# Sums of keys and values stored in whole rows and rearranged later, and two tiles of the last stage weighted and scaled in the third pass

## The chip, the cores and the metric

One core of one Trainium2 chip runs the kernel. The metric is the device time of one execution, in microseconds (us). The engines are TensorE (PE in the profile), VectorE (DVE), ScalarE (ACT), GpSimd (POOL) and SyncE (SP), which issues all the DMAs; SPq is its queue.

## What is computed

```python
x  = A_x                                   # 2048 x 1024
xn = layernorm(x)
q, k, v = split_heads(xn @ wqkv)           # 32 heads of 32
pq, pk  = q @ w_phi, k @ w_phi             # per head
phi_q = concat(softmax(pq), softmax(-pq))  # 64 features a head
phi_k = concat(softmax(pk), softmax(-pk))
kv  = phi_k^T v                            # per head, summed over all rows
z   = sum over rows of phi_k
s   = ((phi_q kv) / (phi_q z + 1e-6)) @ wo
g   = silu((silu(xn @ w1) * (xn @ w3)) @ w2)
out = x + s * g
```

All in float32. A row of `x` needs `kv` and `z`, which are sums over all rows; so the queries' side can only be finished when all keys have been seen.

## The kernel before

The 2048 rows are 16 tiles of 128. The tiles go in eight pairs, `pairs = (0,4), (1,5), (2,6), (3,7), (8,12), (9,13), (10,14), (11,15)`: all large products are done by a recursion that makes the four blocks of a 2 x 2 product from seven products (A11, A12, S2, S1, S3, S4, A22, in this order in the gate and the passes). Each operand is split in a high and a low part, and three products of the parts are added up.

The stages, in order of time:

- **Gate and up** (to about 1180 us): the hidden layer, written to memory as `h_d`. Beside it weights are folded, split and stored.
- **Three passes** (`c` = 0, 1, 2; about 1180 to 1690 us). Passes 0 and 1 make keys and values of half of the heads each, and add up `kv` and `z` in one PSUM bank, `pkv`, by small matmuls (`kv`, L625). Pass 2 makes the queries. For each pair seven operands of 512 KB (`xoA`, `xoS`) are reloaded by `reload` (L521), always one pair ahead. They live in a pool of 11 buffers (`quad`). A pair is seven products of 12 matmuls; bank b is added to by A11, S2, S3 and A22, bank c by S1 and S4, and in between ACT or DVE must have read the partial result.
- `kv_out` (L725) writes out `pkv` when the next pass has got to the product S1 of its first pair: ACT copies the sums of key times value to `kva`, DVE those of the keys to `zs`, and the SP queue stores them in sixteen pieces, eight to `kv_d` and eight to `z_d` (L735, L736), in the order in which the last stage reads them. The stores to `z_d` are element by element, as rows become columns.
- In pass 2, `spikes` (L681) takes a half of a tile's projected queries, subtracts the largest and the smallest of each head (L685 to L689), takes exponents on ACT (L690) and stores the result `e` to `e_d` (L691).
- **Down** (about 1690 to 2234 us): 56 steps (`r`), seven slices of the hidden layer by eight pairs. A step is again seven products, of six matmuls, into banks that DVE, ACT and POOL add to `acc` (L935 to L941). `a_first` and `a_second` load (`hr`, L767) and split (L90, L91) the next step's operands. The other operands (`bo`) come by `load_b` (L760) into a ring of buffers. In the last slice (`end`, steps 48 to 55) each finished pair is gated (`gate`, L870) and stored, and between the steps the first two tiles of the last stage are prepared: `load_e`, `weigh` (POOL, L886, `e` times `z`), `add_up` (DVE, L894), `factors` (L901 to L906) and `scale` (L912, one half on DVE, one on POOL).
- **Last stage** (from about 2234 us): for each tile, `e` scaled is transposed (`turned`, L1036), multiplied with `kvu`, the rearranged sums (L1049), then with `wo` (L1063), and gated and added to `x` (`result`). Tile i+2 is added up and scaled and tile i+3 weighted while tile i is multiplied.

What sets the order: in gate and up, in the last step of down, and in the last stage the order on the engines is the order of the code (`in_order`). In the passes and in most of down the builder orders each engine's instructions ahead of time by its own estimates of when they are ready, earlier code first. The SP queue issues its DMAs strictly one after the other: one that has to wait, for a buffer, for data or for an earlier DMA to land, holds all behind it.

## Time and profile before

| | |
|---|---|
| median of 3 runs | 2474.27 us (2473.87 to 2474.87) |
| the profiled execution | 2471.39 us |
| its span, first to last instruction | 2469.6 us |
| mean granted TensorE clock | 0.994 |
| busy: PE, DVE, ACT, POOL | 2385.4, 1686.7, 901.4, 726.3 us |
| DMA moved | 584.99 MB, mean 237 GB/s |

The profile is of one execution. A row of a timeline gives start and length in us, the engine, the line of the kernel, the operation, output and input by the program's names, shapes and count, and in brackets the time that the engine was idle before and what it waited for. A row of grouped instructions gives, behind the bar, busy us in all and mean ns of one, and behind the second bar the idle time before them. A row of stretches gives start and end, length, the busy time of PE, weight loads, DVE, ACT and POOL with the number of instructions, the granted clock, the share of time in which the DMA engines were busy, and GB/s. The chain of waits gives start, length and what it was that the end hung on. Banks are named banka, bankb, bankc.

### The profile page before, as it was taken

The numbers are of one execution on the slowest core, as the hardware profiler recorded it, in microseconds if no ns is written. First come the engines' busy times: TensorE is split into PE (matmuls) and PEld (weight loads), VectorE is DVE, ScalarE is ACT, GpSimd is POOL, SyncE is SP. The second block draws the span as 40 slices with busy tenths as digits, with TensorE's granted clock in tenths as the row PEclk, the third lists the DMA queues.
The fourth block names the chain that finished last, engine by engine and source line by source line (L and its number), as shares of the span: only waits on it lengthen the run. The fifth ranks groups of instructions, "written<-read, shape, count | busy, mean of one in ns | idle before, by whom it ended". The sixth has DMA issues, their size and how long they took to land.

```text
span 2469.6 us, 35815 instructions
## 1 busy us (share of the span) xinstructions
PE 2385.4 (97%) x13552; PEld 1954.8 (79%) x13552; DVE 1686.7 (68%) x2471; ACT 901.4 (36%) x1564; POOL 726.3 (29%) x521
## 2 busy tenths in 40 slices
PE   6999999999999999999999999999999999989999
PEld 5888877788777887878788788787888888867887
DVE  8656777774476777774576565566678787896764
ACT  6544544443344444543221111234322222333221
POOL 2233455553355555541000000000011111154663
PEclk9999999999999999999999999999999999999999
DMA  7566688866886776775998778897442344556553
GB/s 263 176 223 222 222 279 292 293 227 210 258 282 238 264 260 244 271 242 194 363 353 338 257 246 303 312 352 266 176 169 94 140 178 171 184 187 237 192 186 111
DMA packets 291196, 584.99 MB, mean 237 GB/s; under 512 B 25808, under 2 KB 140496, under 8 KB 288336
## 3 DMA queue, kind: packets, MB, share of 16 engines
q1 hardware_dynamic: 291024, 582.71, 67.6%
q8 instruction: 107, 1.75, 0.3%
q14 instruction: 65, 0.53, 0.1%
HBM read 377.88 MB, written 204.74 MB: 236 GB/s over the span
## 4 chain that ended last, share of the span: by engine, by line
PE 69%; DMA 11%; DVE 7%; issue 6%; POOL 4%; SPq 1%; ACT 1%; DVEq 0%; ACTq 0%; POOLq 0%
PE bankb L556 18%; PE bankb L929 11%; PE bankb L639 9%; PE bankc L556 8%; PE bankc L929 6%; PE banka L556 4%; PE bankc L639 4%; PE banka L929 3%; PE banka L639 2%; POOL ez L886 2%; PE pm L1063 2%; DVE bo L91 2%; DMA xoA<-xo_d0A 1%; POOL e L912 1%; DMA wkv_d0T<-wkvo 1%
## 5 line engine op out<-in xcount | busy, mean ns | idle before, releaser
L91 DVE TENSOR_TENSOR bo<-rw,bo 128x512 fp32r<-128x512 f32 x336 | 295.2, 880 | 146.1 <-ACT bo L90 143.9
L939 POOL TENSOR_TENSOR acc<-acc,u 128x512 f32<-128x512 f32 x48 | 63.8, 1330 | 604.2 <-ACT u L938 604.2
L90 ACT CAST bo<-rw 128x512 fp32r<-128x512 f32 x336 | 205.8, 621 | 48.6 <-PE bankc L556 5.0
L929 PE MATMUL bankb<-bo,as 128*128 128x512 f32 x816 | 201.4, 389 | 2.1 <-DVE acc L941 2.1
L268 POOL TENSOR_TENSOR rw<-rw,t 128x512 f32<-128x512 f32 x56 | 79.3, 1416 | 379.0 <-DVE bo L91 378.9
L1063 PE MATMUL pm<-wos,oT 128*128 128x512 f32 x768 | 182.9, 394 | 0.0
L929 PEld LDWEIGHTS bankb<-bo,as 128*128 128x128 f32 x816 | 153.4, 188 | 34.5 <-DVE acc L941 2.5
L556 PE MATMUL bankb<-op1A,bo 128*128 128x512 f32 x672 | 161.3, 396 | 11.7 <-DVE u L584 8.5
L556 PE MATMUL bankb<-op0A,bo 128*128 128x512 f32 x672 | 160.0, 392 | 8.8 <-DVE u L584 8.4
L1063 PEld LDWEIGHTS pm<-wos,oT 128*128 128x128 f32 x768 | 141.9, 188 | 31.6 <-issue 3.0
L556 PE MATMUL bankb<-op0S,bo 128*128 128x512 f32 x672 | 163.4, 392 | 1.9 <-ACT u L575 1.8
L556 PE MATMUL bankc<-op0S,bo 128*128 128x512 f32 x672 | 163.3, 391 | 2.0 <-ACT u L582 1.4
L556 PE MATMUL bankc<-op1S,bo 128*128 128x512 f32 x672 | 161.8, 390 | 3.1 <-ACT u L582 1.9
L556 PE MATMUL bankb<-op1S,bo 128*128 128x512 f32 x672 | 161.5, 389 | 0.4 <-ACT u L575 0.4
L556 PEld LDWEIGHTS bankb<-op1A,bo 128*128 128x128 f32 x672 | 127.2, 191 | 42.9 <-DVE u L584 12.9
L556 PEld LDWEIGHTS bankb<-op0A,bo 128*128 128x128 f32 x672 | 125.1, 188 | 37.8 <-DVE u L584 11.7
L556 PEld LDWEIGHTS bankc<-op1S,bo 128*128 128x128 f32 x672 | 125.9, 188 | 30.4 <-ACT u L582 2.8
L556 PEld LDWEIGHTS bankb<-op0S,bo 128*128 128x128 f32 x672 | 125.0, 188 | 29.1 <-ACT u L575 3.4
L556 PEld LDWEIGHTS bankc<-op0S,bo 128*128 128x128 f32 x672 | 125.3, 188 | 28.6 <-ACT u L582 1.8
L929 PE MATMUL bankc<-bo,as 128*128 128x512 f32 x576 | 146.6, 389 | 1.4 <-DMA bo<-w_d0B 1.4
L556 PEld LDWEIGHTS bankb<-op1S,bo 128*128 128x128 f32 x672 | 126.1, 188 | 26.9 <-ACT u L575 0.8
L929 PEld LDWEIGHTS bankc<-bo,as 128*128 128x128 f32 x576 | 108.0, 188 | 24.5 <-DMA bo<-w_d0B 1.8
(230 smaller groups left out, 4695.8 us busy)
## 6 DMA issues: line engine op xcount, KB each, us to landing
rw<-in_w SPq DMA_DIRECT2D x112, 512.0 KB, 5.0
h_d<-h SPq DMA_DIRECT2D x112, 256.0 KB, 7.1
hr<-h_d SPq DMA_DIRECT2D x56, 512.0 KB, 3.7
xoS<-xo_d0S SPq DMA_DIRECT2D x48, 512.0 KB, 9.0
xoS<-xo_d1S SPq DMA_DIRECT2D x48, 512.0 KB, 7.4
xoA<-xo_d0A SPq DMA_DIRECT2D x36, 512.0 KB, 9.1
xoA<-xo_d1A SPq DMA_DIRECT2D x36, 512.0 KB, 5.8
e_d<-eq SPq DMA_DIRECT2D x32, 512.0 KB, 5.5
```

The source lines that it names most:

```text
L90: nc.scalar.copy(hi, src)
L91: (by or nc.vector).tensor_sub(lo, src, hi.bitcast(F))
L268: nc.gpsimd.tensor_sub(b11, b22, t2)
L556: nc.tensor.matmul(bank[b], bo[bn][:, w, k], ao[an][:, u, k], start=first and n == 0, stop=LAST[b] == an and n == 11, skip_group_check=True)
L639: nc.tensor.matmul(bank[b], xo[an][:, u, k], wb[bn][:, w, k], start=an in ("A11", "A12", "S1") and n == 0, stop=LAST[b] == an and n == 11, ...
L886: nc.gpsimd.tensor_mul(t, es[i][c], zb[c])
L912: eng.tensor_mul(e3, e3, f.rearrange("p h s -> p (h s)").unsqueeze(2).to_broadcast([P, H, DH]))
L929: nc.tensor.matmul(bank[b], t[:, u, pos + k], bos[kb, bn, k][:, w], start=first and n == 0, stop=LAST[b] == an and n == 5, skip_group_chec ...
L939: nc.gpsimd.tensor_add(c, c, u)
L1063: nc.tensor.matmul(p, oT[k // 4][:, a, k % 4], wos[c, k][:, b], start=n == 0, stop=n == 23)
```

## The change

First, `kv_out` stores whole rows: `kva` in one store to `kv_d[c]`, and the sums of the keys after a transpose on PE (into the free end of the same PSUM bank) and a copy on ACT, in two stores to `z_d` with 32 contiguous numbers each. Sixteen transfers from memory to memory, one in each of steps 8 to 23 of down, bring the sums of key times value from `kv_d` to the order of `kvu_d`, from which `kvu` is loaded, one step later than before (`i == 5`).

Second, the order of tiles in the last stage becomes 3, 9, 0, 1, 2, 4, ... (`TILES`), and the first two, which are the first tiles of pairs 3 and 5, are weighted, added up and scaled in pass 2: `z` is loaded at the beginning of pair 2 into two buffers of the ring, POOL multiplies, and four pieces of vector work (`sum_e`, `sum_ez`, `factors`, `scale`) are queued in `later` and taken up one at each product. Their `e` lies in two other buffers of the ring and is stored when it is scaled. The ring's loads for down that used these buffers (`load_b(0, 2)` and `load_b(0, 3)`, until now in pairs 3 and 4) go to the last pair. The work on the first two tiles leaves the last slice of down; the weighting of the third tile moves from step 55 to the start of the last stage.

```diff
-    kv_d = dram.tile([2, 2, DH, 2 * G, DH], F, name="kv_d")
+    kv_d = [dram.tile([P, 8, DH], F, name=f"kv_d{c}") for c in range(2)]
+    kvu_d = dram.tile([P, 2 * G, DH], F, name="kvu_d")
...
     def kv_out(c, pkv):
         kva = work.tile([P, 8, DH], F, name="kva", tag="w")
         zs = small.tile([P, 8], F, name="zs")
+        zr = small.tile([8, P], F, name="zr", tag="sums")
         nc.scalar.copy(kva, pkv[:, :, :DH])
...
         nc.vector.tensor_copy(zs[:, 4:], pkv[:, 4:, DH])
+        nc.tensor.transpose(zt[0], zs, ident)
+        nc.scalar.copy(zr, zt[0])
+        nc.sync.dma_start(kv_d[c], kva)
         for s in range(2):
-            for j in range(4):
-                sl = slice(32 * j, 32 * j + 32)
-                nc.sync.dma_start(kv_d[j % 2, s, :, G * c + j // 2:G * c + G:2], kva[sl, 4 * s:4 * s + 4])
-                nc.sync.dma_start(z_d[0, c, :, j, s].rearrange("g f -> f g"), zs[sl, 4 * s:4 * s + 4])
+            nc.sync.dma_start(z_d[0, c, :, :, s], zr[4 * s:4 * s + 4].rearrange("g (j f) -> g j f", f=DH))
...
+    def spikes(t, c, p, e, scaling=False):
...
         nc.scalar.activation(e, e, AF.Exp)
-        nc.sync.dma_start(e_d[t][c], e)
+        if not scaling:
+            nc.sync.dma_start(e_d[t][c], e)
+            return
+
+        ef = e.rearrange("p (h f) -> p h f", f=DH)
+        ez = flat(quad("ez", F).rearrange("p u k t -> p (u k) t"))
...
+        nc.gpsimd.tensor_mul(ez, e, early["z"][c])
...
+        def scale():
+            nc.vector.tensor_mul(ef, ef, by.rearrange("p h s -> p (h s)").unsqueeze(2).to_broadcast([P, H, DH]))
+            nc.sync.dma_start(e_d[t][c], e)
+
+        later.extend((sum_e, sum_ez, factors, scale))
+
+    EARLY = (3, 5)
...
-                        if c == 2 and 0 < i < 5:
+                        if c == 2 and i in (1, 2):
                             load_b(0, i - 1)
+                        if c == 2 and end:
+                            load_b(0, 2)
+                            load_b(0, 3)
+                    if later:
+                        later.pop(0)()
...
+    TILES = [pairs[i][0] for i in EARLY]
+    TILES += [t for t in range(NT) if t not in TILES]
...
+        if 8 <= r < 24:
+            c, j, s = (r - 8) // 8, (r - 8) // 2 % 4, r % 2
+            q = 64 * (j % 2) + 32 * s
+            nc.sync.dma_start(kvu_d[q:q + 32, G * c + j // 2:G * c + G:2], kv_d[c][32 * j:32 * j + 32, 4 * s:4 * s + 4])
...
             elif i == 2:
                 load_e(0)
-            elif i == 3:
-                weigh(0, 0, "1")
-                weigh(0, 1, "5")
-                add_up(0, 0)
             elif i == 4:
-                add_up(0, 1)
-                factors_early(0)
                 load_e(1)
                 load_e(2)
+            elif i == 5:
                 kvu = accp.tile([P, 2 * G, DH], F, name="kvu", tag="acc3")
-                nc.sync.dma_start(kvu, kv_d.rearrange("a s f g d -> (a s f) g d"))
-            elif i == 5:
-                scale(0, 0, nc.vector)
-                scale(0, 1, nc.gpsimd)
-                weigh(1, 0, "7")
-                add_up(1, 0)
-            elif i == 6:
-                weigh(1, 1)
-                add_up(1, 1)
-                factors_early(1)
-            elif i == 7:
-                scale(1, 0, nc.vector)
-                scale(1, 1, nc.gpsimd)
-                weigh(2, 0)
-                weigh(2, 1)
+                nc.sync.dma_start(kvu, kvu_d)
...
     load_e(3)
+    weigh(2, 0)
+    weigh(2, 1)
```

More of the change, by code (lines that the diff above doesn't have):

```diff
@@ L626, in kv @@
                                  v[:, 4 * (m % 4) + h], start=first and m == 0, stop=last, skip_group_check=True)
-    pkv = None
+    pkv, zt = None, []
     def seven(xo, wb):
@@ L679, in heads @@
         return pkv, False, last, e1, v1
-    def spikes(t, c, p, e):
+    early, later = {}, []
+    def spikes(t, c, p, e, scaling=False):
         mm = small.tile([P, 2, 16], F, name="mm2")
@@ L690, in spikes, with sum_e, sum_ez, factors @@
         nc.scalar.activation(e, e, AF.Exp)
-        nc.sync.dma_start(e_d[t][c], e)
+        if not scaling:
[3 more added lines that the diff above has]
+        ez = flat(quad("ez", F).rearrange("p u k t -> p (u k) t"))
+        if c == 0:
+            early["s"] = small.tile([P, 2, 2, 16, 2], F, name="sums"), small.tile([P, 2, 16, 2], F, name="by")
+        sm, by, rho = early["s"][0][:, c], early["s"][1][:, c], small.tile([P, 2, 16], F, name="rho")
+        nc.gpsimd.tensor_mul(ez, e, early["z"][c])
+        def sum_e():
+            nc.vector.tensor_reduce(sm[:, 0].rearrange("p h s -> p (h s)"), ef, axis=AX.X, op=OP.add)
+        def sum_ez():
+            nc.vector.tensor_reduce(sm[:, 1].rearrange("p h s -> p (h s)"), ez.rearrange("p (h f) -> p h f", f=DH),
+                                    axis=AX.X, op=OP.add)
+        def factors():
+            nc.vector.reciprocal(rho[:, 0], sm[:, 0, :, 1])
+            nc.vector.tensor_mul(rho[:, 0], sm[:, 0, :, 0], rho[:, 0])
+            nc.vector.tensor_mul(rho[:, 1], sm[:, 1, :, 1], rho[:, 0])
+            nc.vector.tensor_add(rho[:, 1], sm[:, 1, :, 0], rho[:, 1])
+            nc.vector.reciprocal(by[:, :, 0], rho[:, 1])
+            nc.vector.tensor_mul(by[:, :, 1], by[:, :, 0], rho[:, 0])
+        def scale():
[3 more added lines that the diff above has]
+    EARLY = (3, 5)
+    def load_z(two):
+        for c in range(2):
+            nc.sync.dma_start(two[c], z_d[:, c].rearrange("o g j s f -> o (g j s f)").to_broadcast([P, D]))
     def queries(i, xo, wb, steps, pend):
         t0, t1 = pairs[i]
+        if i == EARLY[0] - 1:
+            early["z"] = [flat(bpa.tile([P, 2, 512], R, name="ze", tag=f"ra{6 + c}").bitcast(F)) for c in range(2)]
+            load_z(early["z"])
         for an, pb in seven(xo, wb):
@@ L702, in queries @@
                 e01 = rwp.tile([P, 2, 1024], F, name="eq", tag="rw")
-                spikes(t0, 0, k0, e01[:, 0])
+                if i in EARLY:
+                    early["e"] = [flat(bpa.tile([P, 2, 512], R, name="ee", tag=f"ra{4 + a}").bitcast(F)) for a in range(2)]
+                spikes(t0, 0, k0, early["e"][0] if i in EARLY else e01[:, 0], i in EARLY)
             elif an == "S2":
@@ L841, in tile_kernel @@
             pend = (queries if c == 2 else heads)(i, xo, wb, steps(), pend)
+            assert not (end and later)
             xo = nxt
```

27 lines of the change are left out of this document (13 added, 14 removed).

## The prediction

> **What bounds the kernel now.** I read the page first, then busy time by stretches, then the timelines of the stretches in which TensorE (PE) is not always busy.
>
> ```profile
> PE 2385.4 (97%) x13552; PEld 1954.8 (79%) x13552; DVE 1686.7 (68%) x2471; ACT 901.4 (36%) x1564; POOL 726.3 (29%) x521
> ...
> 1360.00:1525.00 165.00, 158.97 (x1592) 128.74 (x1591) 92.14 (x127) 28.71 (x39) 1.95 (x15) 0.98 0.72 250
> 1525.00:1700.00 175.00, 169.37 (x855) 138.84 (x854) 109.71 (x181) 56.21 (x73) 0.00 (x0) 0.98 0.88 325
> 1700.00:2160.00 460.00, 460.00 (x2030) 380.60 (x2029) 356.07 (x611) 140.43 (x267) 54.81 (x42) 1.00 0.46 167
> 2160.00:2234.51 74.51, 65.02 (x275) 51.75 (x273) 64.81 (x87) 26.94 (x39) 32.82 (x23) 0.98 0.59 206
> ```
>
> Columns: stretch, its length, busy PE, PEld, DVE, ACT, POOL, granted clock, DMA share, GB/s. PE is busy 97% of the span, so only what makes it wait is worth anything. Between 1700 and 2160 it never waits. It is idle for 6.0 us and 5.6 us in the two stretches in which the sums are written out, at a lower granted clock, and for 9.5 us in the end of down. The change touches just these three.
>
> The first two are one story, told by the SP queue:
>
> ```profile
> 1360.00:1370.00 10.00, 9.12 (x162) 7.18 (x160) 4.40 (x8) 2.05 (x4) 0.13 (x1) 1.00 1.00 417
> 1380.00:1390.00 10.00, 10.00 (x106) 8.12 (x105) 6.50 (x9) 2.24 (x3) 0.13 (x1) 1.00 0.09 8
> 1550.00:1560.00 10.00, 10.00 (x46) 8.29 (x45) 1.99 (x4) 2.24 (x3) 0.00 (x0) 1.00 0.15 15
> ...
> 1368.87 0.32 SPq L735 DMA_DIRECT2D kv_d<-kva  x1
> 1372.49 0.30 SPq L736 DMA_DIRECT2D z_d<-zs  x1
> ...
> 1385.68 4.04 SPq L736 DMA_DIRECT2D z_d<-zs  x1
> 1389.82 0.85 SPq L521 DMA_DIRECT2D xoA<-xo_d0A  x2
> ...
> 1389.82 9.06 DMA xoA<-xo_d0A
> 1561.93 7.73 DMA xoA<-xo_d0A
> ...
> 1398.92 5.33 PE L639 MATMUL bankb<-op3B,xoA 128*128 128x512 f32 x12 [5.16 <-DMA xoA<-xo_d0A]
> 1569.80 5.22 PE L639 MATMUL bankb<-op4B,xoA 128*128 128x512 f32 x12 [4.12 <-DMA xoA<-xo_d0A]
> 1575.01 2.72 PE banka L639 x12
> ```
>
> From 1368.87 to 1389.72 the queue issues sixteen small stores, and DMA is busy 9% of 1380 to 1390 and 15% of 1550 to 1560: the queue is stuck, not the memory. The reload of the next pair's operands stands behind them, is issued at 1389.82, lands after 9.06 us, and PE waits 5.16 us. The second time it is issued at 1561.93 and PE waits 4.12 us. After each wait twelve matmuls take 5.33 and 5.22 us where the next twelve take 2.72.
>
> The third is the last round of down:
>
> ```profile
> 2172.87 1.52 PE L929 MATMUL banka<-bo,af 128*128 128x512 f32 x6
> 2182.39 1.52 PE L929 MATMUL banka<-bo,af 128*128 128x512 f32 x6
> ...
> 2218.55 1.52 PE L929 MATMUL banka<-bo,af 128*128 128x512 f32 x6
> 2223.39 2.92 PE L929 MATMUL bankc<-late,as 128*128 128x512 f32 x6 [3.31 <-DVE acc L941]
> ...
> 2233.14 1.53 PE L929 MATMUL bankb<-bo,as 128*128 128x512 f32 x6
> ...
> 2209.62 5.21 POOL L886 TENSOR_TENSOR ez<-e,zb 128x1024 f32<-128x1024 f32 x2 [2.10 <-DVE sums L894]
> 2210.06 2.50 DVE L91 TENSOR_TENSOR as<-s,as 128x512 fp32r<-128x512 f32 x1
> ...
> L894 DVE TENSOR_REDUCE sums<-e 128x32 f32<-128x1024 f32 x4 | 4.8, 1209 | 0.0
> L894 DVE TENSOR_REDUCE sums<-ez 128x32 f32<-128x1024 f32 x4 | 4.8, 1209 | 0.5 <-POOL ez L886 0.5
> L781 DVE TENSOR_TENSOR s<-hr,sm 128x256 f32<-128x256 f32 x5 | 4.6, 924 | 0.0
> L912 DVE TENSOR_TENSOR e<-e,by 128x1024 f32<-128x1024 f32 x2 | 2.4, 1208 | 0.0
> ...
> L781 DVE TENSOR_TENSOR s<-hr,sm 128x256 f32<-128x256 f32 x42 | 17.6, 419 | 0.0
> ```
>
> A step of down is 9.52 us (2172.87 to 2182.39). The next three should put banka at 2210.95; it comes at 2218.55. DVE is why: it carries 12.0 us of adding up and scaling for tiles 0 and 1 (4.8 + 4.8 + 2.4), and its SBUF-only operations stretch while POOL weighs (as<-s 2.50 us, the L781 form 924 ns on average against 419 ns earlier in down).
>
> **The change, part by part.**
>
> *Sums stored whole.* Per write-out, sixteen stores become three: one of whole rows and two of the transposed sums. The fourth store of before goes out at 1372.49, so the queue is free for the reload then, or at the latest 3 × 4.04 us after 1368.87 = 1381.0, if each new store is held as the worst old one. Plus 9.06 us, the operand lands between 1381.6 and 1390.1, and PE needs it at 1398.92 − 5.16 = 1393.76. Both ends are in time. In the third pass the reload also stands behind the pair's own e stores, so it gains less; half of the old hold is enough, as PE was only 4.12 us short. So I take both waits and both slow restarts as gone: 5.16 + (5.33 − 2.72) + 4.12 + (5.22 − 2.72) = 14.4 us. Late next are the operands of the pair's later products, each needed 2.72 us after the one before, from a memory that was idle till now.
>
> *The transpose on PE.* Twice, a product with 128 columns, and a wait for the vector copy of the sums.
>
> ```profile
> L731 DVE COPY zs<-pkv x2: 150/152/153, 1364.1 to 1538.8; 128x4 f32<-128x4 f32 x2
> 1362.21 0.70 PE pkv L625 x59
> 1537.50 0.77 PE L625 MATMUL pkv<-ev 128*32 128x34 f32 x64
> L1036 PE MATMUL pt<-ident,e 128*128 128x128 f32 x256 | 34.1, 276 | 3.0 <-ACT et L1038 2.1
> ```
>
> A transpose is 0.28 us. If PE kept program order it would also wait from the end of the small products to the end of that copy: 1364.25 − 1362.91 = 1.3 us and 1538.95 − 1538.27 = 0.7 us. No order is written by hand in the passes, and the products of S3 are ready, so I expect them to fill the wait: −0.6 us, bounds −0.6 and −2.6.
>
> *Rearranging beside down.* Sixteen memory-to-memory transfers, one in each of steps 8 to 23, in the SP queue ahead of the next step's loads. PE is never idle in that stretch (460.00 of 460.00). No row shows such a transfer. An issue costs 0.30 to 4.04 us by the old stores, in a step of 9.52 us: 0, with a bound of nothing below it, and if the cover went, at most 4.04 us a step.
>
> *Tiles 3 and 9 early, third pass.* Per pair two halves, each with POOL's product, two sums, six small vector operations and a scaling.
>
> ```profile
> 1588.61:1607.65 19.04, 19.04 (x86) 15.77 (x85) 11.69 (x20) 5.26 (x7) 0.00 (x0) 1.00 1.02 407
> ...
> 1586.00 0.69 DVE L714 TENSOR_TENSOR d<-bankb,d 128x512 f32<-128x512 f32 x1 [6.16 <-PE bankb L639]
> ...
> 2246.11 0.35 DVE L901 RECIPROCAL stat<-sums 128x32 f32<-128x32 f32 x1
> 2247.58 0.19 DVE L906 TENSOR_TENSOR by<-by,stat 128x32 f32<-128x32 f32 x1
> ```
>
> DVE works 11.7 us of a pair's 19.04. A half adds 2 × 1.21 + 1.66 (the six from 2246.11 to 2247.77) + 1.21 = 5.3 us, so an early pair asks 22.3, 3.2 too many, and the pair behind it takes them (11.7 + 3.2 = 14.9). PE's tightest call on DVE is L714: it must read S3's bank in the 2.72 us of the product between S3 and A22, and takes 0.69, so 2.0 us of lateness are free. Where it queues behind a POOL product (2.6, half of 5.21) and its sum (1.21), it is 1.8 late beyond that: 4 × 1.8 = 7.2 us at worst, 0 at best. The work is spread one piece a step, so I take 1.5 us, nearer to the stretch's own row, in which PE never waits. Beside POOL, as<-s took 2.50 us instead of about 0.69. The Trainium skill, "SBUF — State Buffer", "Who interferes with whom", makes a rule of it that speaks against this part: a vector instruction with two SBUF inputs and a GpSimd one that reads SBUF take turns for whole instructions. By that rule the subtractions of an early pair are held too, and this term would be the 7.2 of its worst end and the sum 18.4; by the stretch's own row it is 24.1. The two loads of down's operands moved to the last pair come where nothing is reloaded: 0. The loads of z (1 MB in pair 2) come where DMA now has the idle 10 us of 1550 to 1560 in hand: 0; if these are spent, the wait is a reload's and belongs to the rival of the queue.
>
> *Down's end.* DVE loses 12.0 us of work and the stretched operations; PE then keeps its step. From banka at 2210.95 eight products of 1.36 us (9.52 / 7) end at 2221.83; before they ended at 2233.14 + 1.36 = 2234.50. That is 12.7 us. Tile 0's two POOL products now run beside the last step's splits; one stretched operation that delays PE by half of what it is longer than a free one (2.50 − 0.69, L714's row) costs 0.9, so I take 11.8 us (bounds 6.3, if only half comes, and 12.7). The transposes and copies that open the last stage keep their order behind it.
>
> Sum: 14.4 − 0.6 − 1.5 + 11.8 = 24.1 us. The profiled execution took 2471.39 us, 1.8 above its span and 2.9 below the median of the runs, 2474.27; against the median I get 2450.2.
>
> **The rivals.**
>
> *The third pass turns to DVE.* POOL has had nothing to do there (0.00 busy); now its four products stand beside DVE subtractions whose inputs both lie in SBUF. The rows for it are the 2.50 us of L91 beside POOL and the 22.3 us asked of 19.04; against it, that the reductions do not stretch (1209 ns beside POOL's work). Priced above: 7.2 instead of 1.5, so 2455.9. The page's rule named there gives this time; the trace agrees with it in the 2.50 us.
>
> *The queue was not all of it.* The first operands of a pass (2 MB each) are still landing when the reload is issued, and half of the 14.4 us comes back: 2457.4. For it: a DMA share of 1.00 and 417 GB/s up to 1370; against it: 9% right behind.
>
> *Down's end keeps half its wait*, because DVE was late for its own splits as well: 6.3 instead of 11.8, 2455.7. Against it: DVE is 77% busy (356.07 of 460.00) over the 460 us before, and PE waits for nothing.
>
> *Slower: the SP queue stands behind the scaled stores.* Each scaled half is stored from the queue that reloads the operands.
>
> ```profile
> 1597.32 1.15 SPq L521 DMA_DIRECT2D xoA<-xo_d1A  x2
> ...
> xoA<-xo_d1A SPq DMA_DIRECT2D x36, 512.0 KB, 5.8
> ...
> 1607.65 5.44 PE bankb L639 x24
> ```
>
> The reload for the pair that begins at 1610.37 (the second twelve of 24) goes out 13.0 us ahead and lands in 5.8: 7.2 us of slack. If a store that waits for its chain (four vector operations of 0.69, then 2.6, 1.21, 1.66 and 1.21: 9.4 us without the exponent) and for the rest of its pair's vector work (11.7) sits ahead of the reload, that comes 21.1 us late, 13.9 beyond the slack; with a restart of 2.5 that is 16.4 in each of two pairs, 32.8 in all: 2474.3 − (24.1 + 1.5) + 32.8 = 2481.5. It decides from 12.8 us a pair. Against it: the issue order follows estimates of readiness, as e stores and reloads already alternate.
>
> **How the numbers follow.** Forecast 0.69; third pass 0.14; queue 0.07; down's end 0.06; slower 0.04. What measurement can tell is 0.2%, 5 us. The best ends of all terms give 14.4 − 0.6 + 12.7 = 26.5, or 2447.8; with run-to-run differences of 1 us and a little unforeseen I put the low end at 2446. Two of the rivals together (7.2 + 5.7) give 2463.1; I put the high end at 2463. All cases but the last are faster by over 5 us, even three rivals at once (2468.6); about the same would be the last one at half its price. Faster 0.94, same 0.02, slower 0.04.
>
> **What would show it.** Right: no PE idle time put down to xoA in either write-out and DMA share above one half there; the third pass at 19.04 us a pair, pairs 3 and 5 included; banka of down's last four steps 9.52 us apart. Wrong: PE waits for L714, for L706 or for reloads in pairs 3 to 6; DVE still named ahead of PE in down's last round; SP holding hr loads behind the rearranging transfers.

## The result, and the profile after

The changed kernel takes 2457.45 us (median of 4 runs, 2455.73 to 2459.57); the kernel before took 2474.07 (4 runs, 2470.12 to 2474.87) beside it. The ratio is 0.9936, with a 95% interval of 0.9919 to 0.9954, clear of 1: faster, by 16.6 us where 24.1 were forecast. The time is inside the range, and 7 us above the forecast. The profiled execution took 2455.73 us, with a span of 2453.9.

First, busy time by stretches of the changed kernel, for the stretches that were shown of before (the last is cut where down now ends):

```profile
1360.00:1525.00 165.00, 164.01 (x1684) 132.71 (x1683) 98.30 (x136) 29.42 (x40) 1.95 (x15) 1.00 0.77 269
1525.00:1700.00 175.00, 163.40 (x770) 133.54 (x769) 123.96 (x209) 55.60 (x73) 9.59 (x4) 0.97 0.86 318
...
2160.00:2220.00 60.00, 60.00 (x272) 49.76 (x270) 43.39 (x70) 26.21 (x37) 15.68 (x9) 1.00 0.72 254
```

PE's idle time in the first stretch fell from 6.0 to 1.0 us, and in down's end from 9.5 to nothing. But in the second stretch it rose, from 5.6 to 11.6, although the wait at the write-out in it is gone. That is where the missing part of the gain went.

**The write-outs.** The timeline of the changed kernel, the SP queue at both:

```profile
1367.31 0.32 SPq L780 DMA_DIRECT2D kv_d<-kva  x1
1368.60 1.87 SPq L782 DMA_DIRECT2D z_d<-zr  x2
1371.06 2.16 SPq L522 DMA_DIRECT2D xoA<-xo_d0A  x2
...
1533.52 0.32 SPq L780 DMA_DIRECT2D kv_d<-kva  x1
1534.76 1.81 SPq L782 DMA_DIRECT2D z_d<-zr  x2
1537.54 5.07 SPq L696 DMA_DIRECT2D e_d<-eq  x3
1542.70 1.16 SPq L522 DMA_DIRECT2D xoA<-xo_d0A  x2
```

From the first store to the reload it is now 3.75 us (1371.06 − 1367.31), before 20.95 (1389.82 − 1368.87); the second time 9.2 instead of 19.5. No wait for `xoA` is left at either, and no slow restart. The sign that was named for it is there too: from 1380 to 1390 DMA is now busy 78% of the time, where it was 9%.

**Down's end.** The timeline of the changed kernel, the rows of the last steps:

```profile
2179.23 1.52 PE L975 MATMUL banka<-bo,af 128*128 128x512 f32 x6
...
2207.79 1.52 PE L975 MATMUL banka<-bo,af 128*128 128x512 f32 x6
2217.31 1.52 PE L975 MATMUL bankb<-bo,as 128*128 128x512 f32 x6
```

The steps are 9.52 us apart to the end (2179.23 to 2207.79 is three of them); DVE is no longer named ahead of PE.

**The third pass.** The timeline of the changed kernel, one row a pair, PE's only wait there, and the vector operation that POOL's products meet:

```profile
1578.43 2.88 PE L640 MATMUL banka<-op4B,xoA 128*128 128x512 f32 x12
1582.08 3.02 PE L640 MATMUL bankb<-op4T,xoS 128*128 128x512 f32 x12 [0.76 <-ACT k L742]
1587.96 2.40 POOL L704 TENSOR_TENSOR ez<-ee,ze 128x1024 f32<-128x1024 f32 x1 [79.20 <-PE bankc L640]
1588.26 2.12 DVE L715 TENSOR_TENSOR rho<-sums,rho 128x16 f32<-128x16 f32 x1
1598.54 2.88 PE L640 MATMUL banka<-op4B,xoA 128*128 128x512 f32 x12
1600.71 0.18 DVE L715 TENSOR_TENSOR rho<-sums,rho 128x16 f32<-128x16 f32 x1
...
1655.65 2.88 PE L640 MATMUL banka<-op4B,xoA 128*128 128x512 f32 x12
```

From the first to the second banka row it is 20.11 us, and from there 57.11 us for the next three pairs, 19.04 each. PE lost 1.07 us in the third pass's steady part, once.

**The end of the third pass.** What is new is a chain of waits in the last pair. The chain of the changed kernel:

```profile
1652.09 9.82 DMA e_d<-eq
...
1662.03 0.69 DVE eq L692
...
1664.91 7.44 DMA hr<-h_d
...
1673.04 0.79 PE bankb L975
1673.84 4.32 PE bankb L640 x12
```

PE waits 9.07 us for `af`, the first operand of down, which ACT splits from `hr`. One matmul of down stands between the products S1 and S3 of the last pair, in both kernels; PE keeps its order, so S3 waits too, and then restarts slowly (4.32 us for twelve matmuls instead of 2.72). Later PE waits another 1.77 us for `bo`, where before it waited 1.37. The wait, the slow restart and this difference (9.07 + 1.60 + 0.40) make 11.1 us. The SP queue tells why `hr` is late. The changed kernel, then the kernel before, each by its timeline:

```profile
1652.09 5.82 SPq L696 DMA_DIRECT2D e_d<-eq  x3
1657.97 4.25 SPq L803 DMA_DIRECT2D bo<-w_d0T  x4
1664.49 0.32 SPq L696 DMA_DIRECT2D e_d<-eq  x1
1664.91 0.38 SPq L810 DMA_DIRECT2D hr<-h_d  x1
1665.33 7.56 SPq L1019 DMA_DIRECT2D kvu_d<-kv_d  x8
```

```profile
1667.33 2.88 PE L639 MATMUL bankb<-op4B,xoA 128*128 128x512 f32 x12
1672.40 0.38 SPq L767 DMA_DIRECT2D hr<-h_d  x1
1677.30 0.60 ACT L90 CAST af<-hr 128x512 fp32r<-128x512 f32 x1
1678.21 0.39 PE L929 MATMUL bankb<-bo,af 128*128 128x512 f32 x1
```

Before, `hr` was asked for 5.1 us after the last pair's second product began (1672.40 − 1667.33), was split 4.9 us later, and PE got there 10.9 us after that product's start. Now that product starts at 1652.93 (one product of 2.72 ahead of the banka row at 1655.65); the queue first issues the four moved loads and another `e` store that has to wait for its data, so `hr` is asked for at 12.0 us, lands 7.44 us later, and PE starts at 20.1. The difference of 9.2 is the wait. The first rows of the chain tell why that `e` store (1664.49) is late: DVE could write into its buffer only when an earlier `e` store, issued at 1652.09, had landed, and that took 9.82 us (before, the `e` stores of this part took 2.6 to 8.8 us, 3.0 in the median).

Memory was full there before the moved loads came: the DMA share is 1.01 in the 5 us from the second product on (1652.93 to 1657.93), and the loads are issued at 1657.97; at the same place before it is 0.68. One difference stands in the SP queue: five of the seven operands of the last pair's reload now stand behind a scaled store of the early tiles. The changed kernel, then the kernel before, each by its timeline:

```profile
1643.96 0.32 SPq L723 DMA_DIRECT2D e_d<-ee  x1
1644.39 2.38 SPq L522 DMA_DIRECT2D xoS<-xo_d1S  x4
```

```profile
1655.80 2.29 SPq L521 DMA_DIRECT2D xoS<-xo_d1S  x4
```

Counted to the second product, the four `xoS` go out 8.5 us ahead of it, before 11.5 (so also in runs 1 and 5, which keep tiles 0 and 1 in down; in run 2 it is 8.0). PE does not wait for them, but what is issued next shares the memory with them. How much of the late landing is due to this, and how much to the loads, no run tells apart.

The eight `kvu_d` transfers stand here too: eight of the sixteen are issued in the second pass (from 1424.7) and eight from 1665.33, all ahead of down, and not in its steps 8 to 23 as the source says.

I divide the way from the second pair of the first pass to the last stage by four rows of PE that every kernel has: the start of the second `bankb<-op2B,xoA` (before: 1205.04, after: 1203.21), of `banka<-op4B,xoA` in the last pair (1670.05, 1655.65), of the fifth last `banka` of down (2172.87, 2169.71), and of the first `pt<-ident,e` that had to wait (2237.02, 2221.18):

| stretch | before | after | difference |
|---|---|---|---|
| A: write-outs and early tiles | 465.0 | 452.4 | −12.6 |
| B: last pair and down's beginning | 502.8 | 514.1 | +11.2 |
| C: down's end | 64.2 | 51.5 | −12.7 |
| sum | 1032.0 | 1018.0 | −14.0 |

The stages ahead of the first row were 1.8 us shorter in this execution, and the last stage 0.1 longer: with these the span fell by 15.7. The same stretches serve for the experiments. In the fourteen traces the first row starts anywhere from 1202.8 to 1209.3 us, though all changes lie behind it; the stretches leave that out. How much B varies between executions of one kernel is not known, as each has one trace.

### The profile page after: what moved, and what is told of

Same layout as the page of the kernel before. It is cut to its first block, busy times and chain, and to the rows that moved or that the text cites. A ratio compares the mean times of both kernels' runs of the same rounds, so it can differ in the third digit from the quotient of the medians.

```text
span 2453.9 us, 35828 instructions
## 1 busy us (share of the span) xinstructions
PE 2380.6 (97%) x13554; PEld 1951.1 (80%) x13554; DVE 1684.7 (69%) x2493; ACT 902.5 (37%) x1566; POOL 716.9 (29%) x511
## 4 chain that ended last, share of the span: by engine, by line
PE 74%; DMA 9%; DVE 6%; issue 5%; POOL 3%; SPq 2%; ACT 1%; DVEq 0%; ACTq 0%; POOLq 0%
PE bankb L557 18%; PE bankb L975 12%; PE bankb L640 10%; PE bankc L557 8%; PE bankc L975 6%; PE banka L557 5%; PE bankc L640 5%; PE banka L975 3%; PE banka L640 2%; PE pm L1095 2%; DVE bo L92 1%; POOL ez L936 1%; POOL e L962 1%; DMA wkv_d0T<-wkvo 1%; PE pkv L626 1%
## 5 line engine op out<-in xcount | busy, mean ns | idle before, releaser
L557 PE MATMUL bankb<-op1A,bo 128*128 128x512 f32 x672 | 161.2, 396 | 11.5 <-DVE u L585 7.9
L557 PEld LDWEIGHTS bankb<-op1A,bo 128*128 128x128 f32 x672 | 127.2, 191 | 42.4 <-DVE u L585 11.8
L975 PEld LDWEIGHTS bankc<-bo,as 128*128 128x128 f32 x576 | 108.0, 188 | 24.9 <-DMA bo<-w_d0B 2.2
## 6 DMA issues: line engine op xcount, KB each, us to landing
rw<-in_w SPq DMA_DIRECT2D x112, 512.0 KB, 4.7
hr<-h_d SPq DMA_DIRECT2D x56, 512.0 KB, 3.6
xoS<-xo_d0S SPq DMA_DIRECT2D x48, 512.0 KB, 8.7
xoS<-xo_d1S SPq DMA_DIRECT2D x48, 512.0 KB, 7.7
xoA<-xo_d0A SPq DMA_DIRECT2D x36, 512.0 KB, 7.3
xoA<-xo_d1A SPq DMA_DIRECT2D x36, 512.0 KB, 5.8
e<-e_d SPq DMA_DIRECT2D x32, 512.0 KB, 4.3
```

The costliest lines, as they stand in the source:

```text
L557: nc.tensor.matmul(bank[b], bo[bn][:, w, k], ao[an][:, u, k], start=first and n == 0, stop=LAST[b] == an and n == 11, skip_group_check=True)
L975: nc.tensor.matmul(bank[b], t[:, u, pos + k], bos[kb, bn, k][:, w], start=first and n == 0, stop=LAST[b] == an and n == 5, skip_group_chec ...
```

## The experiments

Each was timed beside the kernel before on the same chip (medians of before: 2469.74 for the first four, 2471.43 for the next four, 2471.70 and 2469.10 for the rest). The stretches, in us, from one profiled execution each:

| kernel | time | ratio (95%) | A | B | C |
|---|---|---|---|---|---|
| before | | | 465.0 | 502.8 | 64.2 |
| changed | 2457.45 | 0.9936 (0.9919 to 0.9954) | 452.4 | 514.1 | 51.5 |
| 1 sums only | 2461.54 | 0.9969 (0.9954 to 0.9984) | 451.8 | 506.4 | 64.4 |
| 2 early tiles only | 2468.54 | 0.9989 (0.9975 to 1.0003) | 465.1 | 513.8 | 51.5 |
| 3 transfers pinned | 2458.24 | 0.9954 (0.9939 to 0.9969) | 452.5 | 512.0 | 51.5 |
| 4 hr first | 2452.09 | 0.9933 (0.9917 to 0.9949) | 452.5 | 507.5 | 51.5 |
| 5 keys' sums only | 2458.21 | 0.9955 (0.9939 to 0.9970) | 451.3 | 502.6 | 62.8 |
| 6 whole rows only | 2464.43 | 0.9977 (0.9965 to 0.9990) | 452.0 | 508.3 | 62.8 |
| 7 loads apart | 2454.83 | 0.9942 (0.9922 to 0.9962) | 452.4 | 510.3 | 51.5 |
| 8 hr in pair 6 | 2452.85 | 0.9932 (0.9910 to 0.9954) | 452.8 | 508.5 | 51.5 |
| 9 nothing rearranged, hr first | 2457.60 | 0.9938 (0.9924 to 0.9951) | 452.7 | 513.3 | 51.5 |
| 10 hr first, pinned | 2454.14 | 0.9927 (0.9914 to 0.9940) | 452.8 | 508.1 | 51.5 |
| 11 loads behind hr | 2455.28 | 0.9934 (0.9919 to 0.9950) | 452.7 | 513.8 | 51.5 |
| 12 early tiles of pairs 2 and 4 | 2456.71 | 0.9949 (0.9933 to 0.9966) | 453.2 | 511.5 | 51.5 |

**1 and 2: each part alone.** The first keeps the change's stores and rearranging and leaves tiles 0 and 1 in down; the second keeps the early tiles and the old sixteen stores.

```diff
 # 1: the kernel before, and
+        nc.tensor.transpose(zt[0], zs, ident)
+        nc.sync.dma_start(kv_d[c], kva)
+            nc.sync.dma_start(z_d[0, c, :, :, s], zr[4 * s:4 * s + 4]...)
+            nc.sync.dma_start(kvu_d[...], kv_d[c][...])       # in the steps of down
 # 2: the changed kernel, with kv_out and the load of kvu as before
```

> The kernel before with the first part of the change alone: the sums stored in whole rows, transposed on PE and rearranged by sixteen transfers; tiles and their preparation as before. Theory Q (the new 9 us wait of PE in the last pair of the third pass comes from the SP queue, where the first load of hidden rows for down, hr, stands behind four moved loads and one e store): those loads are not moved here, so both old waits for xoA go (13.6 us with the transposes), the last pair waits under 1 us, and down's end keeps its 12.7 us: ratio 0.9945. Rival T (the wait comes from the rearranging transfers, eight of which were issued directly behind hr and share the memory with it): these are here, so some 8 us of wait come up in the last pair: ratio 0.998. Rival V (the early vector and POOL work makes the exponents and e stores late): as Q here.

> The second part of the change alone: two tiles weighted and scaled in the third pass, the sums still stored in sixteen pieces. Theory Q: the four moved loads and an e store stand ahead of hr again, so PE waits 8 to 10 us in the last pair; the old waits for xoA stay, down's end gains 12.7: ratio 0.999 to 1.000. Rival T: no rearranging transfers, so no such wait, ratio 0.995. Rival V: the wait is there, ratio 0.999 to 1.000.

A falls by 13.2 us with the first part alone, C by 12.7 with the second alone, and C does not move with the first (64.4). B rises by 11.0 with the second part alone, which rearranges nothing. The second ratio is within what was expected of theory Q (0.9989); the first is not (0.9969, expected 0.9945), as B takes back 3.6 of the 13.2. The timeline of the kernel with the second part alone:

```profile
1677.68 1.85 SPq L811 DMA_DIRECT2D hr<-h_d  x3
1685.01 0.79 PE L976 MATMUL bankb<-bo,af 128*128 128x512 f32 x1 [7.69 <-ACT af L90]
```

So the wait for `af` came with the early tiles and the two loads moved for them; the rearranging is not its cause. The first part alone has no such wait, but its B is 3.6 longer as well. The timeline of that kernel:

```profile
1662.30 3.18 SPq L973 DMA_DIRECT2D kvu_d<-kv_d  x5
1683.12 1.65 PE L929 MATMUL bankb<-bo,as 128*128 128x512 f32 x3 [2.69 <-DMA bo<-w_d0T]
```

There the transfers run ahead of down, and PE waits for an operand of down once.

**3: the transfers kept in down.** They are bound to the step's own load, so that they are issued in steps 8 to 23.

```diff
+            with tc.issue_after(hr_load[-1]):
                 nc.sync.dma_start(kvu_d[...], kv_d[c][...])
```

> The changed kernel with the sixteen rearranging transfers kept in steps 8 to 23 of down, each queued behind that step's load of hidden rows, instead of where the builder had moved them (eight in the second pass, eight right behind hr in the last pair of the third). Theory Q: hr is issued as late as before, PE still waits 8 to 9 us, time as the changed kernel (ratio 0.9936, at most 1 us off). Rival T: hr lands 3 to 4 us sooner or more, the wait falls to 5 us or under and the ratio to 0.992 or lower. All: no PE wait in steps 8 to 23.

The sixteen are now issued from 1742.4 to 1885.2 us. B falls by 2.0 us, and the wait for `af` from 9.07 to 7.88. PE never waits in the steps where the transfers now run. So the prediction's price of them (nothing, in those steps) holds where they are in fact issued there. Their early issue is by these traces a small part of the loss; the times do not show it, as this kernel's ratio is 0.9954 and the changed kernel's 0.9936.

**4: hr ahead of the moved loads.** The load of `hr` for down's first step is asked for at the head of the last pair.

```diff
                         if c == 2 and end:
+                            first_h = a_load(0, 0)
                             load_b(0, 2)
                             load_b(0, 3)
```

> The changed kernel with hr's load issued at the head of the last pair, ahead of the four moved loads and of that pair's first e store; all else as changed. Theory Q: hr goes out some 7 us earlier, PE's wait in the last pair falls from 9.1 to under 2 us, and with the restart 8 to 11 us are won over the changed kernel: 2447 to 2450 us, ratio 0.989 to 0.9905. Rival V: the exponents and their stores are as late as before, at least 5 us of wait stay in the last pair, ratio 0.992 or higher. Rival T says nothing certain here, since the transfers move too.

The timeline of this kernel, queue and PE:

```profile
1661.53 0.42 SPq L808 DMA_DIRECT2D hr<-h_d  x1
1668.28 0.74 PE L978 MATMUL bankb<-bo,af 128*128 128x512 f32 x2 [0.79 <-ACT af L91]
1689.57 2.95 PE L978 MATMUL bankc<-bo,as 128*128 128x512 f32 x6 [1.85 <-DMA bo<-w_d0B]
```

The wait falls from 9.07 to 0.79 us, and B by 6.5. The place in the queue was most of it. The time, 2452.09, is above the 2447 to 2450 of theory Q, and B is still 4.7 us longer than before: PE waits 0.79 and 1.19 us for `af` and 1.85 for `bo` (before 1.37), and behind these waits the granted clock is 0.94 and 0.89 from 1681 to 1701, where before it was 1.00.

**5 and 6: which of the sixteen stores held the queue.** On the kernel before: only the sums of the keys transposed, with keys and values still in eight pieces straight to their places; and only keys and values stored whole and rearranged, with the sums of the keys still in eight stores of single elements.

```diff
 # 5
-                nc.sync.dma_start(z_d[0, c, :, j, s].rearrange("g f -> f g"), zs[sl, ...])
+            nc.sync.dma_start(z_d[0, c, :, :, s], zr[4 * s:4 * s + 4]...)
 # 6
-                nc.sync.dma_start(kv_d[j % 2, s, ...], kva[sl, 4 * s:4 * s + 4])
+        nc.sync.dma_start(kv_d[c], kva)
```

> The kernel before, with one half of the write-out changed: the sums of the keys are transposed and stored by two transfers, the products of keys and values still go out in eight small stores straight to their places (ten stores in all instead of sixteen; nothing is rearranged beside down, tiles 0 and 1 stay in down). Theory E, the stores of single elements held the queue: both waits for the operands xoA at the write-outs (5.16 and 4.12 us) are gone or under 1 us, and from the second operand of the first pass to the last stage the time falls by about the 9.4 us of the run with the first part alone. Theory C, it was the count of stores, each alike: with ten of sixteen stores left each wait shrinks by a third to a half, 3 to 5 us gained of the 9.4. If it was the kv stores alone, no gain.

> The kernel before, with the other half of the write-out changed: keys and values stored whole by one transfer and rearranged in memory by sixteen later, the sums of the keys still in eight stores of single elements (nine stores in all). Theory E: the queue is held by the element stores as before, waits of 4 to 5 us and of 3 to 4 us stay, under 2 us gained of the 9.4. Theory C: 3 to 5 us gained, as in the run with the other half. If it was the kv stores alone, the whole 9.4.

Neither theory: each half alone gets nearly the whole of A. The timelines of the two, first write-out (and of the second kernel the one wait that is left):

```profile
1370.74 9.27 SPq L739 DMA_DIRECT2D kv_d<-kva  x8
...
1382.04 0.84 SPq L521 DMA_DIRECT2D xoA<-xo_d0A  x2
```

```profile
1373.65 0.32 SPq L733 DMA_DIRECT2D kv_d<-kva  x1
1374.87 12.08 SPq L737 DMA_DIRECT2D z_d<-zs  x8
1387.07 0.84 SPq L522 DMA_DIRECT2D xoA<-xo_d0A  x2
...
1563.32 3.00 PE L640 MATMUL bankb<-op4B,xoA 128*128 128x512 f32 x12 [1.07 <-DMA xoA<-xo_d0A]
```

Eight stores of pieces hold the queue for 9.3 us, eight of single elements for 12.1, so the two kinds are not far apart. What decides is a threshold. Before, PE needed the operand 24.9 us after the first store (1393.76 − 1368.87), and the reload took 9.06 us; it could wait 15.8 us for its turn, and waited 20.95, which is 5.1 too long, the wait that was seen. With either half changed it waits 11.3 or 13.4 us. At the second write-out 15.4 us were allowed (19.53 − 4.12); the second kernel is at 15.8 (1555.13 − 1539.30), and there PE waits 1.07 us. The landing took 8.05 us there, before 7.73, so the threshold is met to within 0.3 us. Run 5 also needs no rearranging, and its B is that of before (502.6), while run 6, which rearranges, has 5.5 more. On the kernel before, by one trace each, the rearranging bought nothing and went with 3.6 (run 1) to 5.5 us in B; the ratios stand in the same order (0.9955 for run 5, 0.9969 and 0.9977). Why C is 1.4 us shorter in runs 5 and 6 was not tried.

**7 and 8: the two loads in different pairs, and hr a pair earlier.** In both the early weights and the early tiles change rooms, so that in the source the first of the two loads (`load_b(0, 2)`) comes in pair 6 and only the second (`load_b(0, 3)`) in the last. The expectation of run 7 calls them T and B. Both are T (`w_d0T` in the trace; the names T2 and T1 in the source); the operands that PE waits for at the start of down come by the loads issued after the pass, `load_b(0, 4)` to `load_b(0, 6)`, which no run moved.

```diff
-                        if c == 2 and i in (1, 2):
-                            load_b(0, i - 1)
+                        if c == 2 and i in (1, 2, 6):
+                            load_b(0, min(i - 1, 2))
                         if c == 2 and end:
+                            first_h = a_load(0, 0)       # 8: in pair 6, at the fourth product
-                            load_b(0, 2)
                             load_b(0, 3)
```

> The changed kernel with three moves: down's first input hr is asked for ahead of the loads in the last pair, the two early weights take the room of the first of the two deferred operand loads and the early tiles that of the second, and so the first (T) is loaded one pair earlier and only the second (B) in the last pair. Theory Q, the order in the SP queue alone priced the pair's end: no wait for af over 0.8 us, the wait of 1.85 us for the B operand at the start of down gone, 2449 to 2451 us. Theory M, memory time is short and the loads collide wherever they stand: the load in the pair before delays the last pair's operands, PE waits there for xoA or xoS, and the time is that of the run with hr first, 2452, or more.

> As the run before, with hr asked for one pair earlier, in the fourth step of pair 6. Theory Q: the 0.79 us that PE still waited for af with hr first are gone too and nothing else changes, 0.5 to 1.5 us faster than the run with the loads apart. Theory K, what is left is not the queue but ACT's own place for that cast and the buffer that hr needs: the wait stays, or a reload waits behind hr's buffer and PE waits for an operand; equal or slower.

Run 7 contradicts the theory that only the order counts. Its chain of waits:

```profile
1662.33 9.85 DMA hr<-h_d
```

`hr` is asked for 5.1 us after the start of the last pair's second product (1657.25), just as before and as in run 4, and still PE waits 4.58 us, because the load takes 9.85 us to land (before 4.1, run 4: 6.06). So memory time counts as well as the order. The built order again differs from the source: behind the reload's seven operands, the load that was meant for pair 6 is issued at 1651.86 in run 7 and 1653.91 in run 8, 2.7 us before the last pair begins (1654.54 and 1656.62). So the two runs hardly test a load one pair earlier. In run 8 `hr`, meant for pair 6, is issued at 1658.34, early in the last pair, and lands in 11.2 us; no wait for `af` is left in that pair (1.19 us come in down's second step), and B is 508.5 all the same: the waits are now those for the operands `bo` at the beginning of down, as in this row of its timeline:

```profile
1694.33 2.83 PE L980 MATMUL bankb<-bo,as 128*128 128x512 f32 x6 [1.41 <-DMA bo<-w_d0T]
```

**9, 10 and 11: rearranging or loads?** All three start from the changed kernel: keys and values in pieces as in run 5 with `hr` first; `hr` first with the transfers pinned; keys and values in pieces with the loads behind `hr`.

```diff
 # 11
-                        if c == 2 and end:
-                            load_b(0, 2)
-                            load_b(0, 3)
...
                         ready.append(a_first(0, 0) if j == 1 else a_second(*ready[0]))
+                        if j == 1:
+                            load_b(0, 2)
+                            load_b(0, 3)
```

> The changed kernel without the rearranging: the sums of the keys are transposed as changed, keys and values go out in eight pieces straight to their places as before, tiles 3 and 9 stay early, and hr is asked for first in the last pair. Theory R, the rearranging transfers cost 4 to 5 us where they stand between the end of the third pass and the first steps of down (that stretch took 502.6 us in the kernel before and with the transposed sums alone, 506.4 and 508.3 with rearranging, 507.5 with hr first): the stretch comes back to 503 to 504, and the time is 4 us under the run with hr first, 2447 to 2449. Theory L, it is the two moved loads that cost them: the stretch stays at 507 to 508 and the time at 2452.

> The changed kernel with hr asked for first in the last pair and the rearranging kept in steps 8 to 23 of down. Theory R: as above, the stretch at 503 to 504 us and 2447 to 2449, since the transfers then run where TensorE has slack. Theory L: 507 to 508 and 2452, as with hr first alone.

> As the first run of these three, but with hr in its own place and the two loads of down's operands asked for behind it, in the second step of the last pair. Theory Q (only the order in the queue matters): no wait for af, the same time as that run within 2 us. Theory D, a load asked for later lands later: the wait for the operands T or B at the start of down grows to 3 us or more and the run is 2 to 4 us slower than that one.

The theory that the rearranging costs the remaining 4 to 5 us falls: pinned, B is 508.1, no better than the 507.5 without pinning, and with nothing rearranged it is 513.3 and 513.8. That it is the loads fits run 10, but neither theory gave the 513. Of run 11's own theories neither holds: PE still waits 2.56 us for `af`, and B is only 0.5 us longer than in run 9. In run 9 the waits are spread (2.04 us for `af`, 2.05 and 0.65 for `bo`, 1.19 for the next `af`), and its `hr` lands in 7.26 us (run 4: 6.06). Its timeline:

```profile
1669.11 1.22 PE L980 MATMUL bankb<-bo,af 128*128 128x512 f32 x2 [2.04 <-ACT af L90]
```

Runs 9 and 11 are 6 us above run 4 in B, although they issue less there. The traces show where the time goes. The waits that they name in B add up to 5.9 and 6.6 us, in run 4 to 3.8, and behind the waits PE runs more slowly. Busy time by stretches of run 4 and of run 9, in the first steps of down:

```profile
1691.00:1701.00 10.00, 8.68 (x32) 6.03 (x32) 4.17 (x9) 4.63 (x9) 0.00 (x0) 0.89 1.02 415
```

```profile
1691.00:1701.00 10.00, 6.89 (x15) 4.19 (x16) 2.86 (x7) 1.93 (x5) 0.00 (x0) 0.60 0.99 377
```

The granted clock is 0.60 there (run 11: 0.75, run 4: 0.89), and six matmuls behind a wait take 2.90 us in both runs, in run 4 2.12. Why their operands land later stays open: `hr` takes 7.26 and 7.78 us, the `bo` load in the chain 7.99 and 8.24 (run 4: 6.06 and 6.63). Each is one profiled execution, and run 11's, at 2460.46, is 5.2 us above the median of its kernel.

**12: the early tiles one pair earlier.** The tiles of pairs 2 and 4, so that in the source the loads come in pairs 5 and 6 and none in the last; nothing is rearranged, as in runs 9 and 11.

```diff
-    EARLY = (3, 5)
+    EARLY = (2, 4)
-                        if c == 2 and i in (1, 2):
-                            load_b(0, i - 1)
-                        if c == 2 and end: ...
+                        if c == 2 and i in (1, 2, 5, 6):
+                            load_b(0, i - 1 if i < 5 else i - 3)
```

> Sums of the keys transposed, keys and values in eight pieces straight to their places, nothing rearranged. The two early tiles are those of pairs 2 and 4 instead of 3 and 5, so z is loaded in pair 1, the two deferred operand loads come in pairs 5 and 6 (z now holds the room of the first, the tiles that of the second), and hr keeps its own place with no load ahead of it in pair 7. Theory L, what the changed kernel gives back at the end of the third pass is the memory time and the queue's room of the two loads moved into the last pair: the stretch from there to down's steady steps comes back from 514 us to 503 to 505, PE has no wait for af, down's end stays free of waits, and the time is 2446 to 2450 us. Theory Z, the loads collide wherever they stand in this pass: the load of z in pair 1 stands right behind the write-out and the loads in pairs 5 and 6 beside reloads, PE waits 3 us or more for xoA or xoS in pairs 2, 6 or 7, and the time is 2452 or more.

B is 511.5, not 503 to 505, and the wait for `af` 5.44 us. `hr` is asked for 6.2 us after the pair's second product begins and lands in 9.64. But the pair was not clear of the loads. The second one goes out behind the reload, 1.3 us before the last pair begins (1656.29), and takes 12.3 us to land, past the moment at which `hr` is asked for. This is seen in its SP queue, its busy time by stretches (the last figures are DMA share and GB/s) and its chain:

```profile
1655.02 1.51 SPq L805 DMA_DIRECT2D bo<-w_d0T  x2
```

```profile
1651.00:1670.00 19.00, 19.00 (x85) 15.44 (x83) 11.72 (x19) 5.30 (x6) 0.00 (x0) 1.00 1.02 391
```

```profile
1665.16 9.64 DMA hr<-h_d
```

DMA is full there (1.02). The same busy time by stretches of the kernel before and of the changed kernel, each cut at the same place, from 8 us before the last pair's second product to 11 us behind its start:

```profile
1659.33:1678.33 19.00, 19.00 (x86) 15.62 (x84) 12.64 (x21) 7.32 (x10) 0.00 (x0) 1.00 0.77 299
```

```profile
1644.93:1663.93 19.00, 19.00 (x85) 15.43 (x83) 14.12 (x23) 5.94 (x7) 0.00 (x0) 1.00 0.98 351
```

Before, the share is 0.77. While `hr` is under way there it is 0.60 (1672.40 to 1677.30), in run 7 it is 1.02. The figures of theory L did not come, but whether a last pair that is truly clear of the loads gives everything back is not shown. Part of what the other theory said holds, at another place: PE lost nothing to `xoA` or `xoS`, but the loads collided with `hr`.

No version is faster than the changed kernel by more than the intervals of the ratios, which overlap for all that keep both parts. By the traces runs 4, 8 and 10, all with `hr` early, are 5 to 6.5 us shorter in A, B and C together than the changed kernel (1011.5, 1012.8 and 1012.3 against 1018.0); that rests on one profiled execution of each, and runs 7 and 9, with `hr` early too, are 3.9 and 0.6 us shorter. No run moves the two loads without the early tiles.

## Why the prediction was right or wrong

**Sums stored whole: right.** 14.4 less 0.6 for the transposes made 13.8 us; the first part alone took 13.2 off A. The reason holds too (the reload behind the stores), with one correction: the prediction needed sixteen stores to become three, and runs 5 and 6 show that half of them was nearly enough (1.07 us of wait are left in run 6, none in run 5). The two transposes took 270 ns each and PE waited 0.1 us for them in all.

**Rearranging beside down: right about the steps it named, wrong about where it would run.** "One in each of steps 8 to 23" is what the source says; the built order of the queue had all sixteen ahead of down. Kept in those steps they make PE wait for nothing. Issued early they go with 2.0 us in the changed kernel (run 3) and 3.6 without the other part (run 1 beside run 5), by one trace each; with `hr` first, keeping them in those steps gained nothing (508.1 in run 10, 507.5 in run 4).

**Early tiles: right in size, by luck as to the cause.** 1.5 us forecast, 1.07 measured, with all pairs but one at 19.0; the sign "pairs 3 and 5 included" failed for pair 3. The rival of a third pass that turns to DVE (7.2 us) did not come. The collision that it rests on did: the vector product of 128 x 16 that began beside POOL's took 2.12 us, where it takes 0.18 alone. That agrees with the rule of the Trainium skill ("SBUF — State Buffer", "Who interferes with whom") that the two take turns. PE did not wait for it, since it fell on a small operation that nobody waited for soon. The 1.5 us were priced for DVE reading S3's bank late. The 1.07 us are PE's wait for ACT's copy `k` in pair 3, at 1582.08, before POOL's first product begins at 1587.96. There ACT runs an exponent (1580.49, 1.06 us) ahead of the copy, while in the pair before and the two behind it the copy goes first (1559.60, 1598.73, 1617.78). That this order comes from the early work is not shown.

**Down's end: right.** 11.8 forecast, 12.7 measured (run 2 shows the same 12.7 with this part alone), which is the upper bound. The 0.9 put in for a stretched operation did not come.

**The failed step** is in the third pass's term: "The two loads of down's operands moved to the last pair come where nothing is reloaded: 0." Stretch B, in which it lies, took 11.2 us more, against nothing forecast (11.0 in run 2, which rearranges nothing; 9.2 in run 3, where the transfers are kept out of it). The sentence looked for reloads, and there were none; it did not list what else the queue and the memory carried in that pair. The load of `hr`, which down's first matmul needs in the middle of the pair, stood behind the moved loads. The prediction had priced just such a case as its slower rival, a reload that stands behind scaled stores in the SP queue, but not for these loads. Among its signs of being wrong it had `hr` held in the queue, but behind the rearranging; it was held behind the loads, and run 2 shows that it is so without any rearranging. Of the 9.2 us by which `af` came later, 6.9 is the later place (12.0 against 5.1 us after the pair's second product), the rest the longer way from the issue to the split (7.46 us against 4.9). Run 4 shows the first part by giving back 6.5; runs 7 and 12 show the second, by keeping 5.1 or 6.2 and still waiting, with a load in flight. So it is a two-sided cost: putting `hr` ahead removes one side, and no arrangement that was tried removed both. The second side is only in part the loads' own: with the early tiles the last pair's reload goes out 3 us later, behind a scaled store, and memory is full before the loads come. That is the slower rival in a mild form: the stores did come ahead of the reload, and cost no wait for it, but room in memory.

The sum, 24.1, without this step would have been 12.6 + 12.7 = 25.3 from A and C; with it the traces give 14.0 on this way, and 15.7 with the stages outside it. The time still lies in the range because its upper part was opened for rivals of this size, none of which came: the gap from 2450.2 has another cause than the three that were named for it. That the range held is luck as to the cause.

## What to carry to other kernels

A transfer that is moved is priced against everything else in its queue and in memory at the new place, not against the transfers that it was moved away from: list what is issued there, when each is needed and how long it takes to land while DMA is full. A queue's hold costs nothing below the slack of the transfer behind it and everything above; work out the slack first, since half of a rewrite may do. And where a planner orders the queue, read the order that it built before pricing "beside" anything.

## What the hardware showed that was not expected

The same load of `hr` landed 4.1 us after its issue where DMA was busy 60% of its way (before), and took 6.06 (run 4), 9.64 (run 12), 9.85 (run 7) and 11.2 us (run 8) beside other loads, at DMA shares of 1.01, 0.83, 1.02 and 1.02 on the way. Eight stores of 32 rows by four runs of 32 numbers held the queue 9.3 us, eight stores of single elements 12.1: in these two runs the count of stores weighed more than the smallness of their elements. A vector product of 128 x 16 took 0.18 us alone and 2.12 and 1.97 us beside a POOL product of 2.4.
